# A planner that counts the ends of steps, the landings of transfers and the small tiles; the memory read fetched in five pieces; an up tile woven into the output projection

## The chip, the cores and the metric

The kernel runs on one core of one Trainium2 chip. The metric is the device time of one execution in microseconds (us). Times of the kernel before: 1144.30 us at the median of three runs (1142.63, 1144.30, 1148.24).

## The reference

The kernel computes two branches on the same tokens (2,048 tokens of width 640, float32) and mixes them with a gate per token.

```python
g = sigmoid((x * gate_w).sum(-1, keepdims=True))
a = attention_with_memory(x, wq, wk, wv, wo, beta)    # 32 heads of 20, 4 segments of 512 tokens
b = (silu(x @ w1) * (x @ w3)) @ w2                    # 1,728 hidden columns
return g * a + (1 - g) * b
...
# attention, per segment s and head
logits = q_s @ k_s.T * 20 ** -0.5 + causal_mask
a_dot  = softmax(logits) @ v_s
a_mem  = (phi(q_s) @ M) / (phi(q_s) @ z + 1e-6)       # phi(t) = t + 1 for t > 0, exp(t) otherwise
o      = sigmoid(beta) * a_mem + (1 - sigmoid(beta)) * a_dot
M, z   = M + phi(k_s).T @ v_s, z + phi(k_s).sum(0)    # carried to the next segment
```

Segment 0 has an empty memory, so only segments 1, 2 and 3 read it.

## The kernel before

**Two streams.** TensorE has a *dense stream* (projections q, k, v; gate and up products g and u; down products f; output projection op) and *units* of attention: scores with their row maxima (tiles `s`), scores once more with the maximum folded in, then exp (tiles `t`, result `P`), and the product with the values (tiles `o`, one for four heads). The masks of the triangular blocks are applied to `P` by POOL (GpSimd). The chunks 0 and 1 share their weights (called A in the code), and so do 2 and 3 (B).

**Halves of the array.** Each float32 product is made of three float32r products of high and low parts. A dense tile of 128 rows is cut into its rows 0 to 63 and 64 to 127 (`halves`). The first half's matmuls of one tile are issued alternately with the second half's matmuls of an earlier tile, so that both halves of TensorE work side by side.

**What sets the order.** Every instruction of every engine is issued in the order in which the Python program writes it, and the Python program is a planner. It holds a clock for each half of TensorE (`clocks`) and one for each of ScalarE, VectorE and GpSimd (`busy`), and a time at which each of the eight PSUM banks comes free (`until`). `go(e, ns)` books work on an engine; `later(t, f)` calls `f` when the clock reaches `t`; `force` moves the clock on to the next such call; `stages` runs a list of steps one after another. `events` looks after each matmul whether a unit can be issued (three banks free, or two and the unit is late by `LATE` slots), whether a weight is to be loaded or split, and whether a *side* job (`Side`, set up by `braid`) has its turn. Side jobs are short: reads of the memory, transposes, stores.

What the planner before does not hold: the time at which a DMA lands; the number of free buffers of the small tiles `f` (four of 128x512, for SwiGLU and the read) and `hT` (six); SyncE's queue. Stores go into a list (`store_later`, `stores`) and are issued some steps of 700 ns later. A tile counts as made when its last step is written (`done()` in `split`, `hts[c, j] = ht`), not when that step ends. A value product is issued at a fixed slot (`attention`, n == 2), after the units ahead of it are flushed.

**The memory read.** `memory_read` makes tiles `nd` of phi(q) times memory; VectorE divides them into an `f` tile `gm` and SyncE stores it to DRAM (`gd`). `load_memory` loads it back, transposed by 128-token blocks, as one large tile through four DMAs on POOL's queue, and `normalize` multiplies the attention (`oall`) by the reciprocal sums (`spread`, tiles `rr`) and adds the read (`turn`, tiles `gt`, transposes on TensorE). The large tile is the single buffer `big`, which also holds phi(q) of one segment and the raw x of segment 2.

**The output projection.** `oproj` takes `oall` in four blocks of 128 tokens; each is split into high and low parts (`oT`, two buffers) by ScalarE and VectorE; block 2's split starts when block 0's second tile is evacuated. `around` orders: the gate and up tiles of the first chunk of a pair, all eight projection tiles, then the gate and up tiles of the second chunk, with weights loaded once for each.

**Weights.** Each weight block is loaded to `wr`, its high part is made by ScalarE, its low part by POOL (`split`, L169); the first seven blocks by VectorE.

## Time and profile before

| | |
|---|---|
| median of three runs | 1144.30 us |
| profiled execution | 1143.85 us |
| its span, first to last instruction | 1142.1 us |
| TensorE busy with matmuls | 1110.0 us, 97% |
| VectorE (DVE) / ScalarE (ACT) / GpSimd (POOL) busy | 51% / 43% / 51% |
| mean granted clock of TensorE | 0.986 |
| DMA | 156.95 MB, mean 137 GB/s |

In a row of waits stand the engine and line that waited, after `<-` what ended the wait, then us in total, times, and the longest. In a row of the timeline stand start, length, engine, line, operation, out<-in, form and count, and in brackets the idle time of the engine before it and what ended it. A row of a stretch gives busy time and count for PE, PEld, DVE, ACT and POOL, then the granted clock, the DMA engines' share and GB/s. PE is TensorE, PEld its weight loads, SP SyncE.

### The profile page before, as it was taken

The page shows a single profiled execution, that of the slowest core. Times are in us where ns is not written, and L with a number is a line of the kernel's source. Part 1 is how long each engine was busy: PE and PEld are TensorE (multiplying, and loading weights), DVE is VectorE, ACT ScalarE, POOL GpSimd, SP SyncE. Part 2 cuts the span into 40 slices and gives each one's busy share as a digit, 9 for nine tenths or more (in the row PEclk, how much of TensorE's full clock was granted, in tenths as well). Part 3 has the DMA queues.
Part 4 walks back from the last instruction along what each step waited for, and adds up shares of the span by engine and source line. Part 5 has one row for each costly group of instructions (what it writes and reads, how often), then busy time and mean ns, then how long its engine had stood idle before and what let it go on. Part 6 is the DMA issues. An engine that isn't in the chain of part 4 may idle for free. (4 is left out here: it accounts for less than half of the span.)

```text
span 1142.1 us, 29929 instructions
## 1 busy us (share of the span) xinstructions
PE 1110.0 (97%) x11798; PEld 1002.0 (88%) x11798; DVE 583.4 (51%) x1735; ACT 495.7 (43%) x1017; POOL 581.9 (51%) x771
## 2 busy tenths in 40 slices
PE   9999999999999999998999997998999999899998
PEld 7999998889889888987888896887889888788998
DVE  6022564355556643574444764653446654554464
ACT  5255344543443442364656633434542543344230
POOL 5544355455464573533755544634664753665340
PEclk9999999999999999999999998998999989999999
DMA  7454944333343333533787945335544332452111
GB/s 259 152 209 175 283 125 122 83 99 95 96 123 90 98 92 94 166 94 129 214 282 248 311 129 160 108 94 169 149 118 107 111 88 63 134 166 72 61 59 70
DMA packets 88003, 156.95 MB, mean 137 GB/s; under 512 B 19596, under 2 KB 33848, under 8 KB 87864
## 3 DMA queue, kind: packets, MB, share of 16 engines
q1 hardware_dynamic: 56664, 98.59, 26.5%
q0 software_dynamic: 23424, 42.04, 14.9%
q10 hardware_dynamic: 7776, 14.42, 3.5%
q8 instruction: 93, 1.52, 0.5%
q14 instruction: 46, 0.38, 0.1%
HBM read 99.52 MB, written 54.53 MB: 135 GB/s over the span
## 5 line engine op out<-in xcount | busy, mean ns | idle before, releaser
L256 PE MATMUL g<-X,W 64*128 64x512 f32 x1680 | 398.9, 397 | 0.0
L256 PE MATMUL u<-X,W 64*128 64x512 f32 x1560 | 380.8, 397 | 0.0
L1002 DVE CUSTOM_DVE_ANT_0 junk<-s,mask 128x128 bf16<-128x128 f32 (+3 forms) x512 | 250.6, 489 | 223.2 <-PE s L991 183.6
L169 POOL TENSOR_TENSOR W<-wr,W 128x640 fp32r<-128x640 f32 (+1 forms) x139 | 217.3, 1571 | 159.9 <-ACT W L173 157.3
L256 PEld LDWEIGHTS g<-X,W 64*128 64x128 f32 x1680 | 276.4, 186 | 12.9 <-issue 1.0
L1057 ACT ACTIVATE P<-t 128x384 f32<-128x384 f32 (+1 forms) x384 | 181.0, 525 | 227.6 <-PE t L1050 201.2
L256 PEld LDWEIGHTS u<-X,W 64*128 64x128 f32 x1560 | 263.0, 187 | 13.8 <-issue 2.0
L256 PE MATMUL f<-W,ht 64*128 64x320 f32 x2624 | 271.4, 310 | 1.3 <-POOL ht L900 0.9
L256 PEld LDWEIGHTS f<-W,ht 64*128 64x128 f32 x2624 | 252.9, 187 | 5.4 <-issue 1.8
L1066 POOL TENSOR_SCALAR_AFFINE_SELECT P<-P 128x256 f32<-128x256 f32 (+1 forms) x192 | 94.4, 502 | 159.0 <-ACT P L1057 150.5
L173 ACT CAST W<-wr 128x640 fp32r<-128x640 f32 (+1 forms) x144 | 101.3, 727 | 32.7 <-PE f L256 15.1
L256 PE MATMUL op<-W,oT 64*128 64x320 f32 x960 | 100.7, 318 | 4.3 <-DVE oT L169 3.8
L1050 PE MATMUL t<-qk 62*128 62x256 f32 (+2 forms) x512 | 100.3, 331 | 4.3 <-DVE gm L700 4.2
L256 PEld LDWEIGHTS op<-W,oT 64*128 64x128 f32 x960 | 94.0, 193 | 6.2 <-DVE oT L169 5.2
L256 PE MATMUL k<-X,W 64*128 64x512 f32 x600 | 98.5, 401 | 0.0
L256 PE MATMUL v<-W,X 64*128 64x320 f32 (+1 forms) x960 | 95.8, 310 | 0.0
L900 POOL TENSOR_TENSOR ht<-ft,ht 128x512 fp32r<-128x512 f32 x52 | 67.5, 1298 | 55.1 <-ACT ht L904 52.5
L968 POOL DMA_DIRECT2D qk<-qkd x128 | 70.1, 552 | 47.0 <-PE t L1050 25.5
L1012 POOL DMA_DIRECT2D qk<-mr x128 | 73.6, 577 | 39.7 <-DVE mr L1027 21.4
L991 PE MATMUL s<-qk 60*128 60x256 f32 (+2 forms) x512 | 93.1, 325 | 0.0
L256 PEld LDWEIGHTS v<-W,X 64*128 64x128 f32 x960 | 92.3, 186 | 0.8 <-issue 0.6
L938 DVE SCALAR_TENSOR_TENSOR acc<-f,cgate,acc 128x320 f32<-128x320 f32 x128 | 68.7, 546 | 47.1 <-PE f L256 46.5
(118 smaller groups left out, 1349.8 us busy)
## 6 DMA issues: line engine op xcount, KB each, us to landing
qk<-qkd POOLq DMA_DIRECT2D x128, 240.0 KB, 4.0
wr<-in_w_dram SPq DMA_DIRECT2D x86, 320.0 KB
qkd<-qs SPq DMA_DIRECT2D x20, 512.0 KB
qkd<-ks SPq DMA_DIRECT2D x20, 512.0 KB
od<-oq ACTq DMA_DIRECT2D x32, 256.0 KB
wr<-in_wo_dram SPq DMA_DIRECT2D x20, 320.0 KB
vg<-vd SPq DMA_DIRECT2D x16, 336.0 KB
xr<-in_xT_dram SPq DMA_DIRECT2D x20, 256.0 KB
```

The source lines that it names most:

```text
L169: (nc.vector if lo else nc.gpsimd).tensor_sub(dst[:, 1], src, dst[:, 0].bitcast(F32))
L173: stages(bank, ("act", ns, lambda: nc.scalar.copy(dst[:, 0], src)), ("dve" if lo else "pool", 1.4 * ns if lo else 2.15 * ns, low))
L256: ins = nc.tensor.matmul(o, l, x, start=i == 0 and (r == 0 or not w.todo[0]), stop=i == len(todo) - 1 and (r == 1 or not w.todo[1]), skip_ ...
L900: nc.gpsimd.tensor_sub(ht[:, 1], t, ht[:, 0].bitcast(F32))
L938: nc.vector.scalar_tensor_tensor(dst, ps[:, :320], cgate[:, c, lb:lb + 1], dst, op0=ALU.mult, op1=ALU.add)
L968: here(nc.gpsimd.dma_start(t[64 * i:64 * i + RH], qkd[c][RH * (h + i):RH * (h + i + 1)]))
L991: nc.tensor.matmul(ps[i][:, o:o + n], q[:, qb * P:(qb + 1) * P], k[:, :n], start=qb != 1, stop=qb != 0, skip_group_check=True)
L1002: nc.vector.tensor_tensor_reduce(out=junk[:, :n], in0=ps[i][:, o:o + n], in1=mask[:, L - n:], scale=1.0, scalar=-3.0e38, op0=ALU.add, op1= ...
L1012: nc.gpsimd.dma_start(dst, src)
L1050: nc.tensor.matmul(ps[i][:, o:o + L - q0], k[:, kb * P:(kb + 1) * P], q[:, q0:], start=kb != 2, stop=kb != 3, skip_group_check=True)
L1057: nc.scalar.activation(u["P"][:, i, o:o + n], ps[i][:, b:b + n], AF.Exp, scale=SCALE)
L1066: nc.gpsimd.affine_select(d, d, pattern=[[0, 2], [0, n], [1, P]], base=0, channel_multiplier=-1, compare_op=ALU.is_ge, fill=0.0)
```

## The change

1. *Ends of steps.* `split`, `split_psum`, `parts` and the SwiGLU steps report a tile as made when the last step's time has passed (`done` of `stages`). So do the evacuations of `f` and `op` and the masks of `P`.
2. *Landings.* `store_later` issues a transfer at a time `t`, books 400 ns on a new clock for SyncE (or 330 on ScalarE's), and calls a thing landed `LAND` = 4,200 ns later. The rows of maxima count as in 2,700 ns after their DMA. The next use waits for this in the planner: the scores `t` (`fit`), the splits of x, the V tile of segment 2, which reuses the buffer that the stores of segment 0's output read, and whose fill on POOL moves to the opening of the first v tile (`begin_v`).
3. *Small tiles.* Rings for `hT` and `f` (`hold`, `let`, `room`): the planner waits for a buffer as the engine would. `f` has five buffers instead of four and takes over the tile `oq` of the value product; a SwiGLU gate uses one `f` tile instead of two.
4. *The memory read* comes back in five pieces of 128x512, each in an `f` tile, issued on POOL's queue beside the `rr` tiles; a transpose `gt` is opened when its piece counts as landed. `load_memory` and its large tile are gone. The raw x of segments 2 and 3 go through `big` one after the other (segment 3's was loaded early into `hT` and `f` tiles).
5. *`woven`* replaces `around`: of one pair's four gate and up tiles, three come before the projection and the fourth after two of its eight tiles. The weights are loaded once for the pair.
6. *q order:* blocks 3 and 4 of segments 2 and 3 come before blocks 0, 1 and 2 of segment 3.
7. A value product is put into the list of units and waits there for its masks (`fit`), up to the time at which units are issued anyway. The low part of a weight goes to VectorE where POOL's booked time is more than 1.5 us (`SPARE`) later.

```diff
-NST, NW, NRAW, NHT, NVG, NB, FREE = 4, 7, 3, 6, 2, 8, 6
+NFT = 5
+LAND, SPARE = 4200, 1500
...
+            dve, pool = ("dve", 1.4 * ns, sub(nc.vector)), ("pool", 2.15 * ns, sub(nc.gpsimd))
+            return dve if lo or busy["dve"] + dve[1] + SPARE < max(busy["pool"], now()) + pool[1] else pool
+
+        stages(bank, ("act", ns, lambda: nc.scalar.copy(dst[:, 0], src)), low, done=done)
...
-        if units and (free(3) or units[0][0] + LATE < clock["slot"] and free(2)):
+        if units and (free(3) and fit(*units[0]) or units[0][0] + LATE < clock["slot"] and free(2)):
             unit()
...
+    def fit(_, f, p, t):
+        if f is pv_quad:
+            return all(pairs[p + k].get("masked", 0) == 3 for k in range(2))
+        return f is s_unit or pairs[p].get("in") == 2
...
+    def hold(tag, name, e):
+
+        r = rings[tag]
+        while min(r) == float("inf"):
+            if heap:
+                force()
+            elif not lower():
+                raise RuntimeError("no tile for " + name)
+        k = r.index(min(r))
+        busy[e] = max(busy[e], r[k])
+        r[k] = float("inf")
+        holds[name] = r, k
...
-    def store_later(dst, src, key=None, queue=nc.sync, n=5):
-        late.append([n, dst, src, key, queue])
+    def store_later(dst, src, key=None, queue=nc.sync, t=None, done=None):
+
+        e = "sp" if queue is nc.sync else "act"
+
+        def issue():
+            if e == "sp" and busy[e] > now():
+                later(busy[e], issue)
+                return
+            queue.dma_start(dst, src)
+            stored.add(key)
+            later(go(e, 400 if e == "sp" else 330) + LAND, land)
...
+        def fetch(b):
+            t = f_tile(f"gm{c}_{b}", "pool").rearrange("p (q n) -> p q n", n=P)
+            nc.gpsimd.dma_start(t, gd[c][:, :, b * P:(b + 1) * P])
+            later(go("pool", ISSUE) + LAND, lambda: gms.update({b: t}))
...
-        for b in (0, 3, 1, 4, 2):
-            yield spread(b)
-        if c:
-            while c not in gms:
-                yield 1
-            for b in (0, 3, 1, 4, 2):
-                yield turn(b)
+        turns = (0, 3, 1, 4, 2)
+        for i in range(KB + 2):
+            if i < KB:
+                yield spread(turns[i])
+                if c:
+                    while not room("f", 2):
+                        yield 1
+                    fetch(turns[i])
+            if c and i > 1:
+                yield turn(turns[i - 2])
...
-                    flush(lambda: all(p > 2 * m - 3 for _, f, p, _ in units if f is t_unit))
-                    even()
-                    pv_quad(2 * m - 4)
+                    units.append((clock["slot"], pv_quad, 2 * m - 4, 0))
...
+    def woven(cs, j, c):
+
+        plan, key = plan_up([j])[0], ("w", cs, j)
+        floors[key] = plan[0]
+        u = ffn_up(cs, j, plan, free=key)
         o1, o2 = jobs_oproj(c)
-        return o1, o2, a, (7.0, ffn_up(cs[1:], j, plan_up([j])[0]))
+
+        def mix():
+            yield from islice(o2[1], 2)
+            yield from u
+            yield from o2[1]
+
+        return o1, (10.5, islice(u, 3)), (3.5 + o2[0], mix())
```

Three places of the order follow; a number behind a name is that of the buffer's allocation.

The first is POOL at the start of segment 2's v tiles (V2 is the tile of values, `out_0_dram<-acc0` the stores of segment 0's output, P25 the exponentials whose masks the value product of pairs 24 and 25 needs). Before:

```order
L1328 DMA out_0_dram<-acc0_2741 128x640
L1066 AFFINE_SELECT P25_7966<-P25_7966 128x2x128
L1328 DMA out_0_dram<-acc0_2741 128x640
L719 MEMSET V2_8019 128x128
L441 DMA wr70_8040<-in_wqk_dram 128x640
L968 DMA qk1_87<-qkd1_69 60x1024 x2
L1066 AFFINE_SELECT P25_7966<-P25_7966 128x2x128
L1066 AFFINE_SELECT P25_7966<-P25_7966 128x2x256
```

Now:

```order
L1389 DMA out_0_dram<-acc0_2754 128x640 x2
L1135 AFFINE_SELECT P25_7876<-P25_7876 128x2x128
L1135 AFFINE_SELECT P25_7876<-P25_7876 128x2x256
L1034 DMA qk1_87<-qkd1_69 60x1024 x2
L1389 DMA out_0_dram<-acc0_2754 128x640
L478 DMA wr68_8030<-in_wqk_dram 128x640
L1078 DMA qk3_89<-mr_7857 2x4x128 x2
L1135 AFFINE_SELECT P26_8089<-P26_8089 128x2x128
L768 MEMSET V2_8102 128x128
```

The last two masks of P25 stood behind the fill of V2, which needs the stores' landings; they stand ahead of it now.

The second is POOL at the loads of segment 1's memory read (`gm1`). Before:

```order
L169 TENSOR_TENSOR W91_10858<-wr91_10409,W91_10858 128x640
L1148 DMA gm1_10907<-gd1_81 128x640
L169 TENSOR_TENSOR W92_10879<-wr92_10522,W92_10879 128x640
L1148 DMA gm1_10907<-gd1_81 128x640
L968 DMA qk0_86<-qkd2_70 60x1024 x2
L1148 DMA gm1_10907<-gd1_81 128x640
L1066 AFFINE_SELECT P37_10914<-P37_10914 128x2x128
L1148 DMA gm1_10907<-gd1_81 128x640
```

Now, the third to fifth of five pieces (the first is issued 28 rows ahead of these, the second 8):

```order
L1231 DMA gm1_1_11058<-gd1_81 128x4x128
L1078 DMA qk3_89<-mr_10918 2x4x128
L1135 AFFINE_SELECT P38_11048<-P38_11048 128x2x128
L176 TENSOR_TENSOR W92_11062<-wr92_10962,W92_11062 128x640
L176 TENSOR_TENSOR W93_11074<-wr93_10976,W93_11074 128x640
L961 TENSOR_TENSOR ht3_1_11137<-ft3_1_11071,ht3_1_11137 128x512
L1231 DMA gm1_4_11189<-gd1_81 128x4x128
L1135 AFFINE_SELECT P38_11048<-P38_11048 128x2x128
L1135 AFFINE_SELECT P38_11048<-P38_11048 128x2x256
L176 TENSOR_TENSOR W94_11231<-wr94_11150,W94_11231 128x640
L1231 DMA gm1_2_11274<-gd1_81 128x4x128
```

The four loads stood within eight rows; the five pieces are spread over 39 rows.

The third is TensorE behind segment 1's last transposes of the read (`gt1_2`). Before:

```order
L254 MATMUL gt1_2_11158<-ident_84,gm1_10907 128x64
L256 MATMUL g3_1_10954<-X3_8068,W88_10301 128x512
L254 MATMUL gt1_2_11158<-ident_84,gm1_10907 128x64 x3
L256 MATMUL g2_2_11152<-X2_7664,W90_10845 128x512
L256 MATMUL u3_1_11041<-X3_8068,W89_10379 128x512
L256 MATMUL g2_2_11152<-X2_7664,W90_10845 128x512
L256 MATMUL u3_1_11041<-X3_8068,W89_10379 128x512
```

Now:

```order
L263 MATMUL g3_2_11191<-X3_8125,W88_10815 128x512 x13
L261 MATMUL gt1_4_11296<-ident_84,gm1_4_11189 128x64
L1119 MATMUL t39_1_0_11338<-qk3_89 128x384
L1119 MATMUL t39_1_1_11339<-qk3_89 128x384
L261 MATMUL gt1_4_11296<-ident_84,gm1_4_11189 128x64 x3
L261 MATMUL gt1_2_11349<-ident_84,gm1_2_11274 128x64 x4
L263 MATMUL nd3_0_0_11355<-Ms2_0_8896,pq3_9737 128x147
L263 MATMUL nd3_0_0_11355<-Ms2_1_9036,pq3_9737 128x147
L263 MATMUL nd3_0_0_11355<-Ms2_2_9217,pq3_9737 128x84
L261 MATMUL gt1_2_11349<-ident_84,gm1_2_11274 128x64 x4
```

Three rows more of `nd3_0_0` (its second half), and the projection begins with `op1_0_0`. Before, the gate and up tiles of tile 2 (`g2_2`, `u2_2`) stood between the transposes and the projection; now the tiles `g2_2`, `u2_2` and `g3_2` stand ahead of the last transposes.

## The prediction

> **What bounds the kernel now.** I read the page, then TensorE's waits, a table of stretches with the granted clock, and the timeline of each stretch that stands out. All sums are made against the profiled execution, 1143.85 us; the median of the three runs lies 0.45 us above it.

> ```profile
> span 1142.1 us, 29929 instructions
> PE 1110.0 (97%) x11798; PEld 1002.0 (88%) x11798; DVE 583.4 (51%) x1735; ACT 495.7 (43%) x1017; POOL 581.9 (51%) x771
> ```

> TensorE is the bound, with 32 us of the span without a matmul. But 97% hides a second loss: nearly all matmuls use 64 of the 128 rows, so two run side by side. In the timeline:

> ```profile
> 500.18 0.39 PE L256 MATMUL g<-X,W 64*128 64x512 f32 x1
> 500.41 0.39 PE L256 MATMUL g<-X,W 64*128 64x512 f32 x1
> ...
> 516.75 0.31 PE L256 MATMUL v<-W,X 64*128 64x320 f32 x1
> 516.76 0.31 PE L256 MATMUL f<-W,ht 64*128 64x320 f32 x1
> 516.90 0.30 PE L256 MATMUL v<-W,X 64*128 64x320 f32 x1
> 516.91 0.31 PE L256 MATMUL f<-W,ht 64*128 64x320 f32 x1
> ```

> Each half takes a new matmul every 0.23 us (512 columns) or 0.15 us (320 columns), whatever the other does. A stretch with work for one half alone counts as busy and yields half. So I look for three things: idle time, one-sided stretches, and the granted clock. The waits of TensorE:

> ```profile
> PE o L1083 <- POOL P L1066: 8.6, 4, 3.8
> PE gt L254 <- DMA gm<-gd: 7.7, 4, 3.0
> PE t L1050 <- DVE gm L700: 4.2, 1, 4.2
> PE op L256 <- DVE oT L169: 3.8, 4, 1.7
> ```

> These four make 24.3 of the 32 us. Stretches around them, with a quiet one last (after the span of PE come PEld, DVE, ACT, POOL; then the clock):

> ```profile
> 425.00:450.00 25.00, 22.49 (x239) 20.98 (x237) 10.60 (x33) 7.92 (x19) 9.01 (x12) 0.93 0.23 61
> 525.00:550.00 25.00, 24.00 (x291) 22.44 (x293) 12.04 (x39) 12.93 (x29) 9.37 (x14) 0.93 0.42 124
> 700.00:712.00 12.00, 4.71 (x28) 3.85 (x29) 2.06 (x6) 1.26 (x3) 4.73 (x10) 0.65 0.76 233
> 712.00:725.00 13.00, 13.00 (x142) 10.86 (x142) 6.33 (x19) 4.76 (x9) 8.83 (x10) 0.93 0.37 107
> 775.00:790.00 15.00, 13.19 (x131) 10.96 (x133) 5.86 (x22) 6.64 (x13) 10.73 (x13) 0.77 0.49 146
> 935.00:950.00 15.00, 14.31 (x132) 12.33 (x133) 4.66 (x14) 5.42 (x12) 6.54 (x9) 0.77 0.39 95
> 1025.00:1050.00 25.00, 25.00 (x240) 20.88 (x238) 12.10 (x42) 11.79 (x25) 15.21 (x19) 1.00 0.18 50
> ```

> A long wait or one-sided stretch is followed by a lower clock. Busy time times the missing clock is my price: 1.6, 1.7, 1.6 + 0.9, 3.0 and 3.3 us, 12.1 in all.

> **The change part by part.** The matmuls are the same 11,022 program instructions; only their order and what stands ahead of them on POOL, DVE and SP differ.

> *A. Value products wait for masks in the planner* (a product joins the list of small units and is put out when its masks count as done). The longest of its waits:

> ```profile
> 518.46 0.57 POOL L1328 DMA_DIRECT2D out_dram<-acc  x1
> ...
> 523.37 0.38 POOL L719 MEMSET V<- 128x128 f32 x1 [4.34 <-DMA out_dram<-acc]
> ...
> 525.50 1.04 POOL L1066 TENSOR_SCALAR_AFFINE_SELECT P<-P 128x256 f32<-128x256 f32 x2
> ```
> ```profile
> 526.00 2.76 PE L1083 MATMUL o<-P,vg 128*32 128x384 f32 x20 [3.76 <-POOL P L1066]
> ```

> POOL works in order and stood 4.34 us for the landing of a store, with the masks behind it. The order now has these masks ahead of that fill, and the V work waits until the stores count as landed. The other long one:

> ```profile
> 973.15 1.54 POOL L169 TENSOR_TENSOR W<-wr,W 128x640 fp32r<-128x640 f32 x1
> 974.64 1.02 POOL L1066 TENSOR_SCALAR_AFFINE_SELECT P<-P 128x256 f32<-128x256 f32 x2
> ```

> Here a weight split (its low part) stands ahead of the masks; the new order has none between them. The paired work between a quad's last scores and its product grows in the order from 1.9 us at least (3.3 mean) to 2.8 (4.2 mean), at 0.23 and 0.15 us a pair. The added wait has the other units queued behind it, and the dense stream runs on. Bounds: nothing, to 8.6 idle plus 1.7 of clock. I take 7.6 (one short wait stays) and 1.7: **-9.3**.

> *B. The memory read returns in five pieces.* Chain of waits, then the landing of these loads:

> ```profile
> 702.25 6.23 DMA gm<-gd
> ```
> ```profile
> DMA to landing us min/median/max: 3.2/4.0/6.4
> ```

> Before, segment 1's four loads stand on POOL just ahead of the transposes that need them, and the last lands at 708.5. Now each piece (128x512) has an f buffer, its transpose is opened only when the piece counts as landed, and in the order the first piece is issued far ahead. Three more DMA issues on POOL (15 for 12) lie beside other work. Each piece's 512-byte runs are shorter than the old 2,560-byte rows, a landing for which no row exists; between 3.2 and 6.4 I take about 4.0, near the row of like size. Bounds: 5 back if the largest landing recurs, to all 7.7 and 2.5 of clock. I take **-10.2**. [...]

> *C. The planner books the f tiles and landings.*

> ```profile
> 768.59 11.88 SPq L593 DMA_DIRECT2D gd<-gm  x6
> ...
> 776.17 0.49 DVE L700 TENSOR_TENSOR gm<-nd,nd_r 128x320 f32<-128x320 f32 x1 [6.53 <-DMA gd<-gm]
> ...
> 776.81 1.19 PE L1050 MATMUL t<-qk 62*128 62x384 f32 x2 [4.18 <-DVE gm L700]
> ```

> Eight products of the read go through four f tiles; DVE waits 6.53 us for a store, and all behind it with it. With five tiles, one tile less per SwiGLU gate, and the reads of segment 3 spread over the output projection, the wait should go. What is late next is the row maxima behind the products on DVE. Bounds: 0 to 4.2 and 3.0 of clock: **-7.2**.

> *D. An up tile woven into the projection.* Between the first and third pair of projection tiles the order now holds 3.8 to 5.3 us of paired work, where it held 0.3 to 3.5; the fourth pair has 0.9 to 2.3 (1.2 to 2.0 before). So the third pair's waits go and the fourth's stay: of 3.8 us, 2.3, and 0.8 of the 1.6 us of clock: **-3.1**.

> *E. One-sided runs.* The planner now holds work back, and where it does, one half runs alone. Runs of four or more matmuls on one half: 64 with 52.2 us before, 79 with 81.1 us now, priced as above. Half of the excess is 14.4 us; a part replaces waits that other parts would have kept. Bounds 0 (the idle half would have waited) to 28.9 (nothing gained back); I take **+12**.

> *F. The projection starts right behind the normalisation* in segment 1, and nearly so in 3, as it did in 2, since three of the four up tiles are spent earlier. The price is read at segment 2, in the chain:

> ```profile
> 933.77 0.25 PE gt L254 x4
> ...
> 935.49 0.59 DVE oall L1184
> 936.08 0.35 DVE oT L169
> 936.47 3.30 PE op L256 x11
> ```

> From the last transpose to the first product 2.45 us, then eleven products at 0.30 each, which is half rate, and 3.3 us of clock. Bounds: 0, to 5.8 twice. I take one and a little: **+6**. [...]

> *Nothing on the path:* the weights.

> ```profile
> L169 POOL TENSOR_TENSOR W<-wr,W 128x640 fp32r<-128x640 f32 (+1 forms) x139 | 217.3, 1571 | 159.9 <-ACT W L173 157.3 <-issue 1.2
> ```
> ```profile
> L169 DVE TENSOR_TENSOR W<-wr,W x5: 814/906/1228, 17.0 to 20.4; 128x642 fp32r<-128x642 f32 x5
> ```

> The weave loads six weights fewer; 33 splits go from POOL to DVE, which adds 33 x 0.91 = 30 us to DVE's 583 and takes 39 x 1.57 = 61 us from POOL's 582. DVE's half-idle time hides it; without cover each would cost up to 0.91 us. Loading segment 3's x later and the order of the q blocks I cost at nothing: the dense matmuls of v2 and k cover the splits, and the order leaves q3's first block ahead of the heads that need it; uncovered, five x splits at one 4.0 us landing would cost 4.

> Sum: 1143.85 - 9.3 - 10.2 - 7.2 - 3.1 + 12 + 6 = **1132.05, forecast 1132 us**, 1.1% faster.

> **The rivals.**

> *Gain kept whole.* The one-sided runs stand where the other half would have waited anyway, so E is near 2 and F near 3: 1143.85 - 29.8 + 5 = 1119. For it: before, that half's waits cost time that the waits' table does not show. Against: the run of thirteen g matmuls in segment 1 is filler that was paired before.

> *The waits come back elsewhere.* The planner counts 4.2 us for a landing, and rows show 6.23 for a return and 6.53 us of waiting for a store. If half of B and of C returns (8.7 us), the time is 1141, within 0.5% of before, which is about what a measurement tells from no change. The same holds if the planner's clock, without a model of TensorE's clock, drifts off.

> *Slower: VectorE late.* DVE does row maxima, evacuations and projections in order. With 33 splits ahead of row maxima, score banks are freed late and TensorE's small units, then its stream, wait. If each holds TensorE 0.91 us, +30, and 1132 + 30 = 1162; it decides from 11.8 / 33 = 0.36 us each. For it: the splits go to DVE just where POOL is loaded, at the projections, where TensorE already waits for DVE. Against: 49% of DVE's time is free, and the planner moves a split only when DVE is 1.5 us ahead.

> **How the numbers follow.** Forecast's case (1125 to 1138) 0.48; whole gain 0.24; waits elsewhere 0.17; slower 0.11. Faster by over 0.5% (below 1138.6): 0.72; same 0.17; slower 0.11. The range runs from the whole gain's centre, 1119, less a microsecond, to a little past the second rival, 1147; some 0.1 lies above and some 0.08 below.

> **What would show it.** Right for A, if TensorE's wait for masks is below 2 us in all and no fill of V stands on POOL for a store. For B, if no transpose of a piece waits over 1 us and the stretch around 700 to 725 has full clock. For C, if no DVE product waits for a store by over 2 us. For D and F, if the waits for oT move from the third pair to the first, in segment 1 above all, with a lower clock behind them. For E, if TensorE's busy time falls less than its idle time (idle near 12 us, busy still about 1118). Wrong, if idle time falls by 20 us and the span does not: then the one-sided runs took it all.

## The result: 1127.7 us, and the profile after

The changed kernel takes 1127.74 us (median of four runs, 1124.88 to 1132.49); the kernel before, run beside it, 1143.47 (four runs). The ratio is 0.986 with a 95% interval of 0.9815 to 0.9906, so the change gains 1.4%, or 16.0 us of 1143.5. The forecast was 1132. Every other kernel below was also compared with the kernel before on its own chip; I turn the difference between two ratios into time at 1143.5 us each. The interval of the changed kernel alone is 5 us to either side, and this uncertainty stays in every difference against it; with the other kernel's own interval beside it, only the differences of 6.4 and 8.8 us below are clear of zero.

The page of the profile after, its span and the first row of busy times (engine, us, share of the span, instructions):

```profile
span 1122.9 us, 29910 instructions
...
PE 1107.6 (99%) x11798; PEld 997.0 (89%) x11798; DVE 608.5 (54%) x1768; ACT 491.3 (44%) x1011; POOL 532.5 (47%) x735
```

TensorE's waits after (who, on what; us in all, times, longest); the four heads of the list of before were masks 8.6, pieces of the memory 7.7, a product on VectorE 4.2, oT 3.8:

```profile
PE f L263 <- POOL W L176: 2.4, 2, 1.2
PE op L263 <- DVE oT L176: 1.7, 2, 1.4
PE f L263 <- ACT W L181: 1.6, 2, 0.8
PE t L1119 <- DMA qk<-mr: 1.4, 1, 1.4
```

Three of the four old waits are gone from the list. New ones stand in it: f for its weight (4.0 us) and t for its row maxima. The stretches of the prediction, and one more that was quiet before (columns as there):

```profile
425.00:450.00 25.00, 23.09 (x280) 21.01 (x277) 13.12 (x39) 8.50 (x19) 11.39 (x15) 1.00 0.34 92
...
525.00:550.00 25.00, 25.00 (x293) 22.80 (x291) 12.69 (x34) 15.09 (x37) 10.63 (x18) 1.00 0.56 158
700.00:712.00 12.00, 12.00 (x123) 10.65 (x120) 9.62 (x30) 5.05 (x10) 9.44 (x10) 1.00 0.42 127
712.00:725.00 13.00, 11.54 (x88) 10.27 (x86) 7.39 (x19) 5.66 (x14) 5.12 (x9) 0.88 0.36 97
775.00:790.00 15.00, 15.00 (x172) 14.08 (x168) 5.50 (x17) 9.04 (x20) 6.91 (x14) 1.00 0.42 109
...
935.00:950.00 15.00, 15.00 (x189) 14.83 (x189) 9.86 (x33) 7.34 (x17) 9.94 (x14) 1.00 0.28 65
950.00:975.00 25.00, 22.98 (x279) 20.73 (x277) 13.02 (x44) 8.99 (x18) 11.47 (x14) 0.93 0.38 105
```

The stall at 700 has become a smaller one at 718, behind the normalisation of segment 1. The stretch at 775 is whole again. At 950 there is now an idle stretch.

A span can be divided into three parts: idle time of TensorE (span less busy time), time lost to the clock (busy time times the missing clock), and the rest, busy time at full clock. The matmuls are the same (11,798 on both pages), so I read a change of the rest as a change in how much of the work ran on one half alone. Span, idle, clock and busy are those of the one profiled run; the last two columns come from the span and mean clock of every run (of 39 for the kernel before). All in us:

| kernel | median, ratio to before (95%) | span | idle | clock | busy at full clock | span less clock, all runs: median (range) | clock, all runs: median |
|---|---|---|---|---|---|---|---|
| before | 1143.47 | 1142.1 | 32.1 | 15.5 | 1094.5 | 1126.9 (1124.2 to 1130.9) | 14.8 |
| after | 1127.74, 0.9860 (0.9815 to 0.9906) | 1122.9 | 15.3 | 5.5 | 1102.1 | 1116.5 (1114.9 to 1117.3) | 10.1 |
| A undone | 1128.32, 0.9872 (0.9851 to 0.9893) | 1124.6 | 16.3 | 6.6 | 1101.7 | 1117.2 (1115.8 to 1118.5) | 7.9 |
| A and job order undone | 1132.36, 0.9906 (0.9889 to 0.9923) | 1130.1 | 19.9 | 11.1 | 1099.1 | 1119.3 (1118.7 to 1120.2) | 11.3 |
| B undone | 1130.95, 0.9905 (0.9883 to 0.9928) | 1128.2 | 20.1 | 12.2 | 1095.9 | 1117.6 (1115.8 to 1119.2) | 12.4 |
| f tiles not booked | 1125.96, 0.9840 (0.9822 to 0.9859) | 1123.7 | 14.8 | 8.9 | 1100.0 | 1115.6 (1114.7 to 1116.7) | 9.0 |
| weave undone | 1123.95, 0.9839 (0.9817 to 0.9861) | 1123.2 | 14.6 | 10.0 | 1098.6 | 1111.4 (1111.1 to 1113.1) | 10.1 |
| splits on POOL | 1133.25, 0.9916 (0.9892 to 0.9940) | 1131.0 | 14.6 | 8.9 | 1107.5 | 1122.5 (1121.5 to 1123.4) | 9.6 |
| A undone, splits on POOL | 1130.70, 0.9885 (0.9866 to 0.9904) | 1131.5 | 15.9 | 12.3 | 1103.3 | 1120.9 (1118.8 to 1121.7) | 7.9 |
| before, five f tiles | 1140.02, 0.9974 (0.9964 to 0.9984) | 1139.4 | 29.8 | 16.6 | 1093.0 | 1124.1 (1121.4 to 1125.7) | 14.8 |
| before, choice of splits | 1137.90, 0.9948 (0.9932 to 0.9964) | 1134.9 | 28.9 | 11.1 | 1094.9 | 1122.3 (1119.8 to 1123.6) | 14.2 |
| cover behind normalisation | 1124.19, 0.9824 (0.9799 to 0.9849) | 1118.7 | 16.5 | 4.4 | 1097.8 | 1113.8 (1113.0 to 1114.3) | 8.4 |
| up job behind | 1119.57, 0.9783 (0.9766 to 0.9800) | 1117.6 | 12.6 | 4.4 | 1100.6 | 1113.0 (1112.4 to 1113.3) | 4.5 |
| longer landing | 1123.63, 0.9821 (0.9803 to 0.9838) | 1121.3 | 11.9 | 6.7 | 1102.7 | 1114.8 (1113.3 to 1116.3) | 6.7 |

The two columns of all runs take out most of what makes the runs of the changed kernel differ: their times lie 7.6 us apart, their spans less the time lost to the clock 2.4. (The clocks are on record to 0.001, which is 1.1 us of span.) The profiled run of the changed kernel is its fastest, 1124.88 us, and lost least to the clock.

From before to after, in the profiled runs: idle -16.8, clock -10.0, busy at full clock +7.6, together -19.2 us of span. By the medians of all runs, the span without the clock's loss falls by 10.4 us and the loss by 4.7, so half of the 10.0 us of clock is that of one good run. The prediction had 21.8 us of idle time going, and 18 us coming back as one-sided work with its clock (E and F).

### The profile page after: what moved, and what is told of

Read it like the earlier page. It is cut to its first block, busy times and chain, and to the rows that moved or that the text cites. A ratio compares the mean times of both kernels' runs of the same rounds, so it can differ in the third digit from the quotient of the medians.

```text
span 1122.9 us, 29910 instructions
## 1 busy us (share of the span) xinstructions
PE 1107.6 (99%) x11798; PEld 997.0 (89%) x11798; DVE 608.5 (54%) x1768; ACT 491.3 (44%) x1011; POOL 532.5 (47%) x735
## 3 DMA queue, kind: packets, MB, share of 16 engines
q0 software_dynamic: 23664, 42.04, 15.5%
## 4 chain that ended last, share of the span: by engine, by line
PE 96%; DMA 1%; DVE 1%; ACT 1%; POOL 0%; issue 0%; SPq 0%; DVEq 0%; POOLq 0%
PE g L263 18%; PE f L263 17%; PE u L263 17%; PE op L263 7%; PE k L263 7%; PE o L1152 6%; PE v L263 6%; PE q L263 6%; PE t L1119 4%; PE s L1057 4%; PE nd L263 1%; PE pm L263 1%; DMA qk<-mr 1%; DMA xr<-in_xT_dram 0%; PE pkt L261 0%; PE gt L261 0%
## 5 line engine op out<-in xcount | busy, mean ns | idle before, releaser
L263 PE MATMUL g<-X,W 64*128 64x512 f32 x1680 | 393.6, 395 | 0.0
L263 PEld LDWEIGHTS u<-X,W 64*128 64x128 f32 x1560 | 263.0, 185 | 16.3 <-issue 1.8
L263 PE MATMUL f<-W,ht 64*128 64x320 f32 x2624 | 257.7, 309 | 4.0 <-POOL W L176 2.4
L263 PEld LDWEIGHTS f<-W,ht 64*128 64x128 f32 x2624 | 241.5, 186 | 8.2 <-POOL W L176 2.9
L176 POOL TENSOR_TENSOR W<-wr,W 128x640 fp32r<-128x640 f32 (+1 forms) x100 | 158.5, 1590 | 164.0 <-ACT W L181 153.7
L263 PE MATMUL op<-W,oT 64*128 64x320 f32 x960 | 113.6, 315 | 2.5 <-DVE oT L176 1.7
L181 ACT CAST W<-wr 128x640 fp32r<-128x640 f32 (+1 forms) x138 | 97.2, 727 | 39.7 <-PE u L263 17.6
L263 PEld LDWEIGHTS op<-W,oT 64*128 64x128 f32 x960 | 104.4, 189 | 4.1 <-DVE oT L176 2.4
L263 PE MATMUL q<-X,W 64*128 64x512 f32 x540 | 90.8, 396 | 0.0
L263 PE MATMUL v<-W,X 64*128 64x320 f32 (+1 forms) x960 | 90.6, 309 | 0.0
L263 PEld LDWEIGHTS v<-W,X 64*128 64x128 f32 x960 | 87.7, 185 | 0.3 <-issue 0.2
```

Source lines behind the costliest of these rows:

```text
L176: return lambda: e.tensor_sub(dst[:, 1], src, dst[:, 0].bitcast(F32))
L181: stages(bank, ("act", ns, lambda: nc.scalar.copy(dst[:, 0], src)), low, done=done)
L263: ins = nc.tensor.matmul(o, l, x, start=i == 0 and (r == 0 or not w.todo[0]), stop=i == len(todo) - 1 and (r == 1 or not w.todo[1]), skip_ ...
```

## The experiments

### Part A taken back alone

```
-                    units.append((clock["slot"], pv_quad, 2 * m - 4, 0))
+                    flush(lambda: all(p > 2 * m - 3 for _, f, p, _ in units if f is t_unit))
+                    even()
+                    pv_quad(2 * m - 4, 0)
...
-                if keep and (lb, hf) == (0, 0):
-                    begin_v()
...
+        if keep:
+            begin_v()
```

The first v tile no longer asks whether the stores have landed, either.

> The changed kernel with part A alone taken back: a value product is put out at its fixed place again, whatever its masks, and the fill of V's columns stands on POOL ahead of all V work. Theory of the prediction: the waits of o for masks come back (8.6 us, four of them, and 1.7 us of clock; the prediction took 9.3), so 1128 + 9 = 1137 us, with a fill of V that waits some 4 us for a store. Rival: the later store and the other order around v2 alone keep the masks on time; then the masks' waits stay under 2 us in all and the time is 1128 within 2 us.

Measured: 1128.32 us, ratio 0.9872, 1.4 us above the changed kernel and well within the uncertainty. POOL's order in this run, and TensorE's only wait for masks:

```profile
524.32 0.38 POOL L768 MEMSET V<- 128x128 f32 x1 [5.57 <-DMA out_dram<-acc]
```
```profile
PE o L1152 <- POOL P L1135: 1.3, 1, 1.3
```

The fill of V stands on POOL for a store, longer than before the change (5.57 us, 4.34 before), and no product is late for it: the product near it was already out at 515.6, and its masks stood ahead of the fill. So the rule did not remove the long wait. Something else had moved the fill away from the masks of a product.

### Part A and the order of the jobs around v2

The change also moved whole jobs here: the stores of the output and all of d1 now stand ahead of v2, where half of d1 had been woven into v2. My prediction had this in A's text but gave it no term of its own. Beside the edit above:

```
-    seg += [(0, load_raw(3)), braid(d1, out0, 700), braid(v2, (0, x3), 3000, 2000)]
+    seg += [(0, load_raw(3)), braid(take(d1, 4), out0, 700), braid(braid(v2, d1, 2400), (0, x3), 3000, 2000)]
```

> Part A taken back as before, and also the order of the jobs around v2: four tiles of d1 beside the stores of the output, the other four woven into v2 beside x3, as in the kernel before. Theory: what removed the long wait of o24 was the order of the jobs (the stores now go out some 10 us ahead of the V work), not the rule that products wait; with the old order the fill of V waits for a store with masks behind it and a product waits 3 us or more, 1128 + 5 = 1133 us. Rival: the masks are still in time, under 2 us of waiting in all, 1128 us within 2.

Measured: 1132.36 us, ratio 0.9906, 5.3 us above the changed kernel. POOL, then TensorE:

```profile
522.82 0.37 POOL L768 MEMSET V<- 128x128 f32 x1 [7.84 <-DMA out_dram<-acc]
...
525.55 1.05 POOL L1135 TENSOR_SCALAR_AFFINE_SELECT P<-P 128x256 f32<-128x256 f32 x2
```
```profile
526.06 2.77 PE L1152 MATMUL o<-P,vg 128*32 128x384 f32 x20 [5.90 <-POOL P L1135]
```

The chain of the kernel before is back, step by step: store, fill, masks, product. Without the clock's loss this run is 2.8 us above the changed kernel, and the ranges do not meet. So with the new order of the jobs the old rule was good enough, and with the old order it is not: the order carried this part of A. Whether the old order with the new rule would show the same wait was not run.

### All low parts of weights on POOL

```
-            return dve if lo or busy["dve"] + dve[1] + SPARE < max(busy["pool"], now()) + pool[1] else pool
+            return dve if lo else pool
```

> The changed kernel, but every low part of a weight (except those that were on DVE before) is made on POOL, as before the change: some 33 splits at 1.57 us go back from DVE at 0.91. Theory of the prediction: the choice costs and brings nothing, 1128 us within 2. Rival 1 (VectorE late, the slower case of the prediction): DVE freed of 30 us makes it faster, 1122 or below. Rival 2: POOL with 52 us more holds back masks and low parts, o or f wait for POOL by 5 us more, 1133 or above.

Measured: 1133.25 us, ratio 0.9916, 6.4 us above the changed kernel. The row of busy times:

```profile
PE 1116.4 (99%) x11798; PEld 1007.6 (89%) x11798; DVE 580.9 (51%) x1735; ACT 491.1 (43%) x1011; POOL 577.4 (51%) x768
```

Idle time is not higher than after (14.6 against 15.3); TensorE's busy time is, by 8.8 us. Of these, 5.4 us are busy time at full clock, and without the clock's loss all runs together are 6.0 us above the changed kernel (1122.5 for 1116.5, ranges apart). As I read it, the planner takes POOL to be late, holds work back, and a half runs alone meanwhile; that reason is argued from the code, not shown. Such a loss shows in no table of waits.

### The choice of the engine alone, in the kernel before

The lines of `split` that choose the engine, put into the kernel before.

> The kernel before with the choice of engine for the low parts of weights alone: the planner gives one to DVE when DVE would end it 1.5 us sooner. Theory of the prediction: nothing on the path, 1143.5 us within 2. Rival 1, from the run with all low parts on POOL (5 us slower, with 8.8 us more of busy time of TensorE and no more idle time): a POOL that is freed lets the planner put out weights and masks sooner, fewer runs of one half alone (44 us instead of 52 in the order), 1138 us. Rival 2 (VectorE late): slower, 1148 us or more.

Measured: 1137.90 us, 0.9948 (0.9932 to 0.9964): 5.9 us faster, with an interval that leaves out no change. That is the first rival's figure, but not its mechanism: the busy time at full clock, where runs of one half alone would show, is that of before (1094.9 for 1094.5), and idle time is 3.2 us less. TensorE's wait for masks in this run, where before it was 8.6 us in four:

```profile
PE o L1089 <- POOL P L1072: 3.3, 2, 1.9
```

So the choice of engine also takes 5.3 of the 8.6 us of waits for masks: two are left of four, the longest of 1.9 us instead of 3.8. The wait of t for the product on VectorE, C's 4.2 us in one, is 0.3 us here. VectorE, 39 us busier, holds t and s anew in five waits, of 1.8, 0.9, 0.6, 0.4 and 0.4 us, 4.1 us in all, about what went with that wait. The slower rival of the prediction has no support.

### Both together

> Part A taken back as in the run that undid it alone (there a fill of V waited 5.57 us for a store on POOL, and yet the products waited only 1.3 us for masks), and all low parts on POOL as in the run that did that alone. Theory: two things keep the masks on time, each enough alone, the planner's rule and a POOL freed of 33 splits; with both gone the products wait for masks by 5 us or more, and the time is 1133 + 6 = 1139 us. Rival: neither, the masks are on time because the order around them moved for another reason; the masks' waits stay under 2 us and the time is that of the splits alone, 1133 us within 2.

Measured: 1130.70 us, ratio 0.9885, and 1.6 us of waits for masks in all. The expectation of 1139 failed: with both gone the masks are in time, and the run is not slower than the one with the splits on POOL alone. The order of the jobs, which this run kept, is what is left to keep them in time. The idle time is 1.3 us more than with the splits alone, the one-sided work 4.2 us less: orders as different as these shift some us between the parts for no reason that I can name.

### Part B taken back alone

The four loads into one tile, `load_memory` at its old places, and transposes that ask for nothing.

```
-            later(go("pool", ISSUE) + LAND, lambda: gms.update({b: t}))
...
-            return Work(f"gt{c}_{b}", parts, evac, ready=lambda: b in gms)
+            return Work(f"gt{c}_{b}", parts, evac)
...
+    seg = [braid(braid(braid(chain(main + [ua]), r, 2000, 0), (0, gm), 700, 0), o1, 1500, 3000),
```

> The changed kernel with part B alone taken back: the memory read returns in four loads through one large tile, put out when its products' stores have been put out, and the transposes do not ask whether it has landed. Theory of the prediction: 7.7 us of waits for the loads and 2.5 us of clock return, 1128 + 10 = 1138 us. Rival: in the changed kernel the stretch 700 to 725 still has 1.46 us idle, a clock of 0.94 and halves that run alone, so most of the stall was only moved from the loads to the projections behind the normalisation; with the old loads the projections come later and find their data ready, and the time is about 1131 us (3 us more).

Measured: 1130.95 us, ratio 0.9905, 5.1 us above the changed kernel: between the two. The waits, then two stretches:

```profile
PE gt L261 <- DMA gm<-gd: 7.3, 4, 4.0
```
```profile
690.00:696.00 6.00, 0.73 (x2) 0.36 (x2) 0.12 (x1) 0.00 (x0) 1.57 (x4) 0.56 0.85 225
...
712.00:725.00 13.00, 13.00 (x126) 12.82 (x124) 10.42 (x32) 5.20 (x12) 6.70 (x8) 1.00 0.29 88
```

The waits are those of before, 7.3 us for 7.7. But 712 to 725, where the changed kernel waits for oT, is whole: the transposes end earlier in this order, and 11.3 us of work stand between them and the first projection. So a part of what the pieces gain is given back right behind them. In the profiled runs, undoing B adds 4.8 us of idle time and 6.7 of clock (2.3 by the medians of all runs), and takes away 6.2 us of one-sided work. Over all runs it adds 1.1 us without the clock's loss, with ranges that overlap: what B gains as a whole is not clear of the noise.

### The f tiles without the planner's book

```
+        if tag == "f":
+            return
         r = rings[tag]
...
+        if name not in holds:
+            return
```

> The changed kernel with the five f tiles, but without the planner's book of them: it takes one whenever it wants one (the engines then wait in the program for the tile to come free), and a read or a returned piece does not wait for room. Theory of the prediction (C's 7.2 us come from the booking): DVE products wait for stores again by over 2 us and TensorE behind them, 1135 us. Rival: the fifth tile and the one tile less per gate carry the gain alone, 1128 us within 2.

Measured: 1125.96 us, ratio 0.984: the rival. VectorE's wait for a store, then TensorE's for VectorE:

```profile
DVE gm L750 <- DMA gd<-gm: 3.1, 1, 3.1
```
```profile
PE t L1123 <- DVE gm L750: 0.6, 1, 0.6
```

A product does wait for a store again, and TensorE waits 0.6 us for it. A copy of a value product on ScalarE, which takes one of these tiles too, also comes late and holds TensorE for 1.7 us, once; the changed kernel has no such wait. The time does not rise by it. The book is not what carries C.

### The five f tiles alone, in the kernel before

```
-        ot = sp.tile([P, L], F32, tag="oq", name=f"oq{p}", bufs=1)
+        ot = f_tile(f"oq{p}")
...
-        return sp.tile([P, L], F32, tag="f", name=name, bufs=4)
+        return sp.tile([P, L], F32, tag="f", name=name, bufs=5)
...
-                u = f_tile(f"fu{c}_{j}")
+                u = f_tile(f"fu{c}_{j}") if half else t
```

> The kernel before with the tiles of part C alone: the tile of the value product's copy joins the ring of f, which has five buffers, and a SwiGLU gate multiplies in place (one f tile instead of two). TensorE's order is that of the kernel before, instruction by instruction. Theory of the prediction in its size, with the tiles as its carrier (the run without the book showed that the book carries nothing): the product's wait of 6.53 us on DVE goes, and with it 4.2 us of TensorE and 3.0 us of clock around 775: 1143.5 - 7.2 = 1136 us. Rival: the row maxima or the next store are late in its place and the stretch stays as it is, 1143.5 us within 2.

Measured: 1140.02 us (12 runs), 0.9974 (0.9964 to 0.9984): 3.0 us faster. VectorE's wait, then the stretch that had a clock of 0.77:

```profile
775.37 0.49 DVE L700 TENSOR_TENSOR gm<-nd,nd_r 128x320 f32<-128x320 f32 x1 [3.94 <-DMA gd<-gm]
```
```profile
775.00:790.00 15.00, 14.00 (x186) 12.43 (x188) 6.22 (x24) 7.59 (x15) 9.39 (x12) 1.00 0.63 191
```

TensorE's order is that of before, so the two traces differ by the tiles alone. VectorE still waits for a store, 3.94 us instead of 6.53; the wait of t for the product is gone, and a wait of f for VectorE of 2.3 us stands in its place. The clock of the stretch is back at 1.00, but not that of the run: it loses 16.6 us as a whole, for 15.5 before (14.8 in both at the median of all runs), with 0.88 in 950 to 975, a stretch further on. So the mechanism was right, five tiles shorten the stall, and its size was not: 3.0 us of the 7.2, and the 3.0 us of clock among them did not come back. In the changed kernel the stall is gone altogether; there four of the last five products of the read stand some 3 us apart (at 749.33, 752.66, 755.21 and 758.21), so that the tiles come round in time.

### The weave taken back (D, E and F)

```
-        u = ffn_up(cs, j, plan, free=key)
+        a = 7.0, ffn_up(cs[:1], j, plan_up([j])[0])
         o1, o2 = jobs_oproj(c)
...
-        return o1, (10.5, islice(u, 3)), (3.5 + o2[0], mix())
+        return o1, a, chain([o2, (7.0, ffn_up(cs[1:], j, plan_up([j])[0]))])
```

> The changed kernel with the woven up tile taken back in segments 0 to 2: the up tile's two halves of the chunks stand ahead of and behind the projections, its weights loaded twice (six loads more), the projections in one run. Theory of the prediction: D's 3.1 us are lost and F's 6 us are gained where the projections have cover again, so 1128 + 3.1 - 6 = about 1125 us, with waits for oT at the third pairs. Second theory, from the trace of the changed kernel: the weave also brought a new wait, of f for its weight (2.4 + 1.6 us, at 448 and 955), which goes as well: 1121 us. Rival: the weave is worth D and more, since the order of this kernel has no cover ahead of the first projection of segments 1 and 2 here either: 1131 us or over.

Measured: 1123.95 us, ratio 0.9839, 2.4 us below the changed kernel: near the first theory in time. Without the clock's loss it is 5.1 us below, and the ranges do not meet. Two waits and two stretches:

```profile
PE gt L261 <- DMA gm<-gd: 3.3, 1, 3.3
PE op L263 <- DVE oT L176: 2.2, 2, 1.4
```
```profile
712.00:725.00 13.00, 10.46 (x55) 9.95 (x56) 4.40 (x14) 3.29 (x9) 2.23 (x4) 0.53 0.21 54
...
950.00:975.00 25.00, 25.00 (x299) 23.11 (x299) 14.23 (x45) 9.46 (x21) 14.50 (x19) 1.00 0.43 118
```

The waits of f for a weight, at 448 and 955 after, are not in this list, and 950 to 975 is whole. In exchange a piece of the memory is late in segment 1, and 712 to 725 has a lower clock than in any other run. The waits for oT stand near the first projections, at 718 and 920, not at the third pairs as the theory had it. Idle time is much the same as in the changed kernel; what falls is the busy time at full clock, by 3.5 us. So the weave costs something as a whole, and the reason is in part one that the prediction did not see. TensorE's timeline of the changed kernel shows it:

```profile
448.49 0.41 PE L263 MATMUL f<-W,ht 64*128 64x320 f32 x1 [0.81 <-ACT W L181]
448.49 0.41 PE L263 MATMUL op<-W,oT 64*128 64x320 f32 x1
450.11 0.41 PE L263 MATMUL f<-W,ht 64*128 64x320 f32 x1 [1.21 <-POOL W L176]
```

The ring of weights has seven buffers; five hold the projection's. The up tile used to stand behind the projections, and its matmuls covered the splitting of the down tiles' weights. Now f follows op at once, its third weight finds a buffer only when the last projection tile frees one (ScalarE starts on it at 447.71, after a wait of 1.44 us for op), and both halves stand through the split, 0.81 us for ScalarE and 1.21 for POOL.

### Cover behind the normalisation

```
         def mix():
+            yield from islice(u, 1)
             yield from islice(o2[1], 2)
             yield from u
             yield from o2[1]
-        return o1, (10.5, islice(u, 3)), (3.5 + o2[0], mix())
+        return o1, (7.0, islice(u, 2)), (7.0 + o2[0], mix())
```

> The changed kernel with one edit: of the four tiles of the woven up tile two stand with the normalisation (three now), one between the normalisation and the first pair of projections, one between the second half of that pair and the next tile. In the order this leaves 0.6 to 3.3 us of work ahead of the first projection in segment 1 (0 to 0.3 now) and 3.0 to 3.9 in segment 2 (0 now). Theory of the prediction (F, priced at 6 us, is real and comes from missing cover): the wait of op for oT and the low clock behind it in segments 1 and 2 shrink, 1128 - 4 = 1124 us or less. Rival: the normalisation ends later by the tile that it lost and the stall moves with it: 1128 us within 2.

Measured: 1124.19 us, ratio 0.9824, 4.1 us below the changed kernel, the theory's figure but within the uncertainty; without the clock's loss 2.7 us below, with ranges apart. The six runs fall into two groups, three of 1120.4 to 1121.8 us with clocks of 0.995 and 0.996 and three of 1126.6 to 1128.5 with 0.989 and 0.990, and the profile is of the first. Segment 2, and a wait in segment 1:

```profile
900.00:925.00 25.00, 24.80 (x263) 21.70 (x259) 16.64 (x51) 12.35 (x27) 14.64 (x21) 1.00 0.50 133
925.00:950.00 25.00, 25.00 (x300) 22.78 (x292) 14.03 (x48) 9.83 (x22) 14.16 (x20) 1.00 0.31 76
```
```profile
PE gt L261 <- DMA gm<-gd: 3.3, 1, 3.3
```

No wait for oT is left in the list, and in segment 2 the clock stays at 1.00 in this run. In segment 1 the rival holds as well: with a tile less beside the normalisation a piece of the memory is late by 3.3 us.

### One up job behind the projections

The edit above, and one of the two whole up jobs of segments 0 and 2 moved behind the projections; the normalisation's units closer together:

```
-    seg = [braid(chain(u + [ua]), o1, 1800, 4000), ub, job_down(A, 3)]
+    seg = [braid(chain(u[:1] + [ua]), o1, 1800, 4000), ub, u[1], job_down(A, 3)]
...
-    seg = [braid(braid(chain(main + [ua]), r, 2000, 0), o1, 1500, 3000),
+    seg = [braid(braid(chain(main + [ua]), r, 2000, 0), o1, 1000, 3000),
...
-    seg = [braid(chain(u + [ua]), o1, 1800, 2500), ub, job_down(B, 2),
+    seg = [braid(chain(u[:1] + [ua]), o1, 1000, 0), ub, u[1], job_down(B, 2),
```

> The cover of the run before, and besides: in segments 0 and 2 one whole up job is moved from ahead of the normalisation to behind the projections, ahead of the down tiles, and the normalisation's units may follow each other after 1.0 us of dense work instead of 1.8 (segment 2) and 1.5 (segment 1). Theory (the changed kernel's new wait of f for its third weight, 4.0 us at 448 and 955, comes from weights that find a free buffer only when the projections end): the moved job gives these weights time, the wait goes, and with the cover the time is 1128 - 4 - 4 = 1120 us. Rival: the moved job's own weights now meet the full ring of seven, or the normalisation is late by the job that it lost, and the time is 1126 us or over.

Measured: 1119.57 us, 0.9783 (0.9766 to 0.9800): faster than both kernels, 8.8 us below the changed one by the ratios. The head of its list of waits:

```profile
PE gt L261 <- DMA gm<-gd: 3.7, 2, 2.3
PE t L1119 <- DMA qk<-mr: 1.3, 1, 1.3
```

No wait of f for a weight, none of op for oT: both waits went as the theories had it. The gain has another make-up than 4 and 4. Without the clock's loss this run is 3.5 us below the changed kernel and only 0.8 below the run with the cover, since 2.8 us of one-sided work came in where 3.9 of idle time went; the rest is clock, which all four runs kept at 0.995 or 0.996. What is left is a wait for pieces in segment 2, where the shorter stretch ahead of the projections now ends with the transposes.

### A longer landing in the planner's book

```
-            later(go("pool", ISSUE) + LAND, lambda: gms.update({b: t}))
+            later(go("pool", ISSUE) + 7000, lambda: gms.update({b: t}))
```

> The version with the up job behind the projections, and one number more: a returned piece counts as landed 7.0 us after its issue instead of 4.2 (in that version two transposes waited 3.7 us for pieces, in segment 2). Theory: these waits go and the stretch behind them keeps both halves busy, 1119.6 - 4 = about 1116 us. Rival: the planner holds the transposes back and runs one half alone meanwhile, so that the wait is only renamed, 1119.6 us within 2.

Measured: 1123.63 us, ratio 0.9821, 4.3 us above the run without it. The waits stay:

```profile
893.33 1.26 PE L261 MATMUL gt<-ident,gm 64*128 64x64 f32 x8 [2.19 <-DMA gm<-gd]
896.15 0.66 PE L261 MATMUL gt<-ident,gm 64*128 64x64 f32 x4 [1.55 <-DMA gm<-gd]
```

The theory fails: the waits neither went nor became others. As I read the code, the planner has no other dense work left at that place, so it steps over the landing in its own book, whatever its length; that is argued, not shown, and where the 4.3 us come from (2.3 of clock and 2.1 of one-sided work by the table) I did not trace. The run with the cover alone has dense work beside the transposes of segment 2 and no such wait there; that combination was not run.

## Why the prediction came out

The forecast was 1132.05, the measurement 1127.74, within its range and with its sign. The terms were less good than their sum: that errors of some 4 to 6 us in the weights, A, B, C and E nearly cancelled is luck. The rival of the whole gain, 1119, and the slower one did not happen. By step:

*Weights, taken at 0: wrong, the largest miss.* The step "DVE's half-idle time hides it" looked at one side, what 33 splits cost VectorE, and there it held. That POOL was freed of 61 us was put at nothing since no row showed TensorE waiting for a split. Measured: 5.9 us faster alone in the kernel before, 6.4 slower when undone. In the kernel before the gain shows in waits, of masks that no longer stand behind a split and of the product on VectorE; in the changed kernel it is one-sided work, 5.4 us, and no wait.

*A, -9.3: the waits went as described, by another cause.* Masks 8.6 to 0, and the fill of V waits 0.60 us for a store, where the prediction wanted none. The step that gave all of it to the rule (a product joins the small units) failed: undone, it cost 1.4 us, within the uncertainty. The order of the jobs around v2 and the choice of engine can remove most of it without the rule; rule and order together are worth 5.3 us by the ratios and 2.8 without the clock's loss.

*B, -10.2: right in mechanism, 5.1 us measured, with an uncertainty as large.* No transpose waits for a piece in the changed kernel, and undone, the waits came back as 7.3 us of the 7.7. The pieces landed in 3.3, 3.6 and 7.1 us (least, median, longest), at the median near the 4.0 that it took. The sign of full clock from 700 to 725 failed: it was 0.94. The step that failed is the addition of B, E and F as separate terms: with the stall of B back, the projection behind it has its cover, so undoing B also undoes F in segment 1, and 6.2 us of one-sided work go with it.

*C, -7.2: right in mechanism, 3.0 us for the tiles alone, nothing for the book.* The step that failed is the heading, "the planner books the f tiles"; the tiles and the spacing of the reads did it. No product waits for a store in the changed kernel, as forecast.

*D, -3.1, and F, +6: right in sign and place.* Together +2.9; the weave undone gained 2.4 (5.1 without the clock's loss, in which some of E is included). The wait for oT did move to the first pair, in segment 1 above all: 1.7 us in two waits, 1.37 of them at 720. With cover behind the normalisation the time fell by 4.1 us (2.7 without the clock's loss), some half of F's price; no run shows the rival's F of near 3 by itself. Missing was the work late next: f's third weight, 4.0 us idle.

*E, +12: too large.* All one-sided work, E's and that in F, shows as 7.6 us more of busy time at full clock. I had counted runs of four or more in the order. The forecast of 1118 us of busy time failed (1107.6): 10.0 us of clock came back at the same time in the profiled run, 4.7 in the median. Idle time ended at 15.3 for 12, by the new waits.

The gains by experiment are 5.3 (A with its order), 5.1 (B), 3.0 (C) and 5.9 (choice of engine), and the weave costs 2.4: 16.9 us beside 16.0 measured. That the two agree so well is partly luck, since each difference against the changed kernel is uncertain by some 5 us, and A, B, C and the choice of engine overlap. The later load of x3 and the order of the q blocks were not run by themselves.

## What to carry to other kernels

Where an order is planned by a model of the engines, price what an edit frees as well as what it loads: a less loaded side engine was worth some 6 us here, in one kernel by shorter waits and in the other by one-sided work that no table of waits shows. Split each run's time into idle time, clock and the rest before comparing two kernels, since the clock differs from run to run (mean clocks of 0.989 to 0.995 in the four runs of the changed kernel). Ahead of crediting a rule with a wait that went, look whether whole jobs moved at the same place. Work that stands between a producer and its consumer is cover; count it on both sides of whatever is woven in, the buffers that it holds included.

## What the runs showed of the chip

In the traces of the two kernels the lower clock stands behind idle times of 0.49 us and more, though not behind every one, and never behind one-sided work without idle time. Slices of 2 us, first of the changed kernel, then of the kernel before (columns as in the stretches):

```profile
714.00:716.00 2.00, 2.00 (x12) 1.57 (x11) 1.08 (x6) 0.58 (x2) 1.65 (x3) 1.00 1.02 283
...
718.00:720.00 2.00, 0.66 (x7) 0.39 (x5) 1.93 (x7) 1.26 (x4) 0.25 (x1) 1.00 0.03 8
720.00:722.00 2.00, 1.97 (x13) 1.97 (x14) 1.25 (x3) 0.01 (x1) 0.00 (x0) 1.00 0.23 82
722.00:724.00 2.00, 2.00 (x16) 2.00 (x15) 0.00 (x0) 0.00 (x0) 0.00 (x0) 0.50 0.12 30
```
```profile
932.00:934.00 2.00, 2.00 (x14) 1.63 (x13) 1.52 (x6) 1.14 (x3) 1.59 (x3) 1.00 1.09 312
934.00:936.00 2.00, 1.51 (x10) 1.07 (x8) 1.89 (x3) 0.95 (x3) 1.53 (x3) 0.91 1.11 250
936.00:938.00 2.00, 1.80 (x8) 1.53 (x7) 1.76 (x5) 1.75 (x4) 0.05 (x1) 0.50 0.19 25
938.00:940.00 2.00, 2.00 (x11) 2.00 (x11) 0.02 (x1) 0.00 (x0) 1.60 (x2) 0.50 0.00 0
```

At 714 one half works alone (12 matmuls in 2 us) at full clock. Then come 1.34 us without a matmul (718 to 720), and from 722 on the clock is 0.50. In the kernel before, 0.49 us of idle time (934 to 936), beside one-sided work, stand ahead of the fall at 935.66. The long rows that read less than 1.00 (0.77 for 935 to 950 before, 0.88 for 712 to 725 after) are means over stretches of 1.00 and 0.50.

```profile
718.59:722.00 3.41, 2.04 (x14) 1.97 (x14) 2.59 (x8) 1.23 (x3) 0.00 (x0) 1.00 0.15 53
722.00:725.41 3.41, 3.41 (x25) 3.41 (x25) 0.00 (x0) 0.87 (x2) 0.38 (x1) 0.50 0.32 99
725.41:728.82 3.41, 3.41 (x46) 3.36 (x45) 1.38 (x4) 0.00 (x0) 2.43 (x5) 1.00 0.64 145
```

Counted in such steps, the one ahead of each of the eight falls had between 0.49 and 3.35 us of idle time (932.25 and 522.65 in the kernel before). In these two traces a step without idle time was never followed by a fall, not even the least filled behind the first 30 us, 916.56 to 919.97 in the changed kernel, in which 16 matmuls start where the median of all such steps is 36. Other steps of up to 1.91 us kept the full clock, and a wait of 3.33 us, which lay across the border of two steps, cost no clock at all (kernel before, two steps and the one behind):

```profile
969.79:976.62 6.83, 3.50 (x36) 1.12 (x36) 0.00 (x0) 0.00 (x0) 6.81 (x10) 1.00 0.64 168
976.62:980.04 3.42, 3.42 (x39) 3.42 (x41) 2.06 (x9) 1.93 (x4) 0.15 (x1) 1.00 0.45 136
```

So these traces give no threshold: one step with 0.49 us of idle time was followed by a fall, and one with 1.91 us was not. Nor do they show a price of one-sided stretches in clock, which the prediction put beside that of long waits: the one-sided slice at 714 kept its clock at 1.00, and each of the eight falls has idle time in the step ahead of it. The row of 935 to 950, with a clock of 0.77, has those 0.49 us ahead of its fall at 935.66, with one-sided work beside them.
